# Order of the tail projections at the start of a segment-recurrent attention kernel, and a cap on the filling work of a step

## Chip, core and metric

The kernel runs on one core of one Trainium2 chip. The metric is the device time of one execution in microseconds (us). Before the change three timed runs gave 980.9, 981.39 and 983.57 us, so the median is 981.39 us.

The engines are named as in the profile: PE is TensorE (PEld its weight loads), ACT is ScalarE, DVE is VectorE, POOL is GpSimd, and SP is SyncE, which here does nothing but issue DMA transfers. PSUM is the memory that PE accumulates into; DVE and ACT copy ("evacuate") results from it to SBUF, the working memory.

## What is computed

Part A is attention with a memory that is carried from segment to segment. The sequence has 2048 tokens of 640 values, cut into 64 segments of 32. Each segment's 32 tokens stand behind 8 memory rows; the output of those 8 rows is the memory of the next segment. Part B is a dense layer with a squared ReLU. Layer norms and residuals stand around both.

```
mem = mem0                                   # 8 rows of 640
for s in range(64):
    h = concatenate([mem, xs], axis=1)       # 8 + 32 rows, xs = layernorm(x) of segment s
    q, k, v = h @ Wq, h @ Wk, h @ Wv         # 32 heads of 128
    scores = where(mask, q @ k.T * scale, -1e9)
    o = softmax(scores) @ v @ Wo
    mem = o[:, :8]
    outs.append(o[:, 8:])
h = x + concatenate(outs)
out = h + relu(layernorm(h) @ w1 + b1) ** 2 @ w2 + b2
```

Weights and activations are bfloat16, sums are float32.

## The kernel before

**Steps, blocks and tails.** A step is one segment; a block is four of them (128 tokens), so there are 16 blocks and 64 steps. A step's memory rows and its first 24 tokens are one group of 32 rows, projected inside the step (`step`, `proj`). The last 8 tokens of the four segments of a block form another group of 32 rows, the block's tail. Tails don't depend on the recurrence, so they can be projected at any time before their block: `tail_units(b, which)` cuts the projection of block b's tail by Wq, Wk or Wv into ten units of four matmuls, five for each half n of the heads. The last unit of a half hands out `tail_out`, the evacuation. The output projection of a block's tail rows is cut into ten units too (`wo_tail_units`).

**Evacuation and rows.** `tail_out` copies the half from PSUM to a row of 512 values per partition. A query or key half takes a row buffer from `rowtile` (four buffers, shared with the projections of the steps) and leaves a flip (a DVE transpose) in the list `late`, which frees the row. A value half is written to DRAM (`vt_d`) by a DMA transfer on SP, and its buffer is free when that transfer has landed. At the start 18 other places stand ready for value halves in the list `parked` (tiles that are needed only later, plus `parkx`), some with their writes put off in the list `writes`; value halves that find `parked` empty take a row buffer. Block 0's value halves take row buffers too and are written by POOL's queue. With blocks 1 to 9 parked, those of blocks 10 and 11 take row buffers.

**The start.** `start` streams Wv, Wq and Wk as they arrive, with tail units between the chunks. In the stream of wq and right behind it run the value units of blocks 4 to 7, 40 units. In the stream of wk run 30 units and right behind it ten more: value units of blocks 8 to 11. What is left in `units`, the tail queries and keys of block 1, goes into the list `fill` for step 0. All loads of weights stand on SP's queue in the order Wv, Wq, Wk, Wo (lines 114 and 149), and the writes of the parked values behind them.

**Step 0.** `step` runs with `ready` set: its projections are done already, by `start`. After the scores it runs ten units of `fill` and all flips in `late`, then the values and the copies of their result into oT. Wo comes in eight pieces, and the output rounds (`wo_rounds`, tile pw) of step 0 are in four parts that each need two pieces. `SEG0` says how many units of `fill` run ahead of each of the four parts. `wo_out` and `mem_to_hT` (line 374) then make the memory rows of the next step.

**Filling the later steps.** Ahead of each step `portion(s)` takes units from a plan that is sorted by due step. It aims at eight units a step on average from step 2 on (`n = round(8.0 * (s - 2)) - paced[0]`), always takes what is due, and can take only what is ready: when too little was ready in earlier steps, n is larger and a later step gets more than eight. The units run at four places of the step: one or two ahead of the memory's values, two behind them, two behind the output rounds, and the rest behind the token values, ahead of the next step's first projection.

**Semaphores of SP.** In the built program the transfers on SP use eight completion semaphores in turn, and each issue waits for the transfer eight issues before it.

Of the kernel before, what the change touches and what calls it, by code (L numbers as in the profile page):

```python
# [16 lines left out]
def kernel(  # L17
# [151 lines left out]
    def rows_of(b, sp):  # L169
        at = HD + sp * SEG  # L170
        return lambda c: hTs[b % 2][:, c * CW + at:c * CW + at + SEG]
# [15 lines left out]
    def ln_norm(b):  # L187
        mv, rs = xns[b]
        xn = s1.tile([128, D], BF16, tag="xn", name="xn")
        xt = xts.pop(b)  # L190
        nc.vector.tensor_scalar(out=xn[:], in0=xt[:], scalar1=mv[:, 0:1], scalar2=rs[:, 0:1],
                                op0=ALU.subtract, op1=ALU.mult)
        xns[b] = xn
# [28 lines left out]
    def proj(w, by, lhs, n, ps, c0, c1):  # L222

        if by == "columns":
            wr = w[:].rearrange("p (c g j n k e) -> p c n k g j e", c=DC, g=G, n=2, j=4, k=4)
        elif by == "half":
            wr = w[:].rearrange("p (c k j n e) -> p c n k j e", c=DC, k=G, n=2, j=4)
        else:
            wr = w[:].rearrange("p (c k n f) -> p c n k f", c=DC, k=G, n=2)
        for c in range(c0, c1):  # L230
            for k in range(4):
                nc.tensor.matmul(ps[32 * k:32 * k + 32, :], lhsT=lhs(c), rhs=wr[:, c, n, k], start=(c == 0), stop=(c == DC - 1))  # L232

    def mmtile():
        return mm.tile([128, 512], F32, tag="mm", name="ps")
# [4 lines left out]
    def evac(dve, out_, in_):  # L240
        if dve:
            nc.vector.tensor_copy(out=out_, in_=in_)  # L242
        else:
            nc.scalar.copy(out=out_, in_=in_)  # L244

    def rowtile():
        return s2.tile([128, 512], BF16, tag="row", name="row", bufs=4)
# [12 lines left out]
    def wo_rounds(lhs, pw, hs):  # L260

        for h in hs:
            for kh in range(2):
                for ch in range(2):
                    j = kh * 2 + ch
                    p = kh * 16 + h
                    c0 = 32 * (1 - kh)
                    nc.tensor.matmul(pw[32 * j:32 * j + 32, c0:c0 + DH], lhsT=lhs(p), rhs=wov2[:, head(p), ch],  # L268
                                     start=(h == 0), stop=(h == 15))
# [18 lines left out]
    def run(q, n, held=None, stop=False):  # L288
        while n > 0 and q:
            out = q.pop(0)()  # L290
            if out and held is not None:
                held.append(out)
                if stop:
                    break
            elif out:
                out[1]()
            n -= 1
# [15 lines left out]
    def tail_rows(b, c):  # L313
        return hTts[b // 4][:, c, b % 4].rearrange("p k s -> p (k s)")

    def tail_units(b, which):
        w = {"q": wq, "k": wk, "v": wv}[which]
        lhs = lambda c: tail_rows(b, c)
        st = {}

        def unit(n, c):
            def f():
                if c == 0:
                    st[n] = mmtile()
                proj(w, "columns" if which != "v" else "order", lhs, n, st[n], c, c + 1)
                return (True, lambda: tail_out(b, which, n, st[n][:])) if c == DC - 1 else None
            return f
        return [unit(n, c) for n in range(2) for c in range(DC)]

    def tail_out(b, which, n, ps, dve=False):  # L330
        row, wait = parked.pop(0) if which == "v" and 0 < b and parked else (rowtile()[:], False)
        evac_row(which, row, ps, dve)
        if which == "v":
            eng = nc.sync if b else nc.gpsimd

            def write():
                eng.dma_start(out=vt_d[b, 2 * n:2 * n + 2].rearrange("j r f -> r j f"),
                              in_=row.rearrange("r (j f) -> r j f", j=2))
            if wait:
                writes.append(write)  # L340
            else:
                write()
            return
        if n == 0:
            tails.setdefault(b, {})[which] = s2.tile([128, H, 32], BF16, tag=which + "Tt", name=which + "Tt")
        dst = tails[b][which]
        late.append((0.71, lambda: flip(row, dst, n), 4 * b - (which == "k")))
# [97 lines left out]
    def step(b, sp, v=None):  # L445
# [199 lines left out]
        if not last:  # L645
            pw = chn.tile([128, 512], F32, tag="ch", name="pw")
            if ready:
                for k in range(4):
                    run(fill, SEG0[k])
                    wo_rounds(lambda p: oT[:, p, M:NK], pw, [2 * k + h + 4 * (k // 2) for h in (0, 1, 4, 5)])  # L650
# [72 lines left out]
    parked += [(hnT0[:, c, :], True) for c in range(DC)] + [(ht0[k][:, 0:512], True) for k in range(NK4)]  # L723
    parked += [(t, True) for t, _ in halves(oTts[1][:].rearrange("p h r -> p (h r)"))]
    writes = []
    SEG0 = (0, 0, 8, 8)
    hnTs = [hnT0[:], ck(DC * NT).rearrange("p (c t) -> p c t", c=DC)]
    ots = [ck(D) for _ in range(4)]
    fxs = [ck(D) for _ in range(4)]
# [45 lines left out]
    def start():  # L775

        v = s2.tile([128, EG], BF16, tag="v", name="v")
        main = rows_of(0, 0)
        pas = [pop.tile([128, 2, 512], F32, tag="po%d" % h, name="pa%d" % h) for h in range(2)]
        banks = [pas[h][:, n, :] for h in range(2) for n in range(2)]  # L780
        banks += [mmtile()[:] for _ in range(3)] + [chn.tile([128, 512], F32, tag="ch", name="pv")[:]]
        for c in range(DC):
            for k in range(4):
                for n in range(2):
                    proj(wv, "order" if k else "half", (lambda c, b=k - 1: tail_rows(b, c)) if k else main, n,
                         banks[2 * k + n], c, c + 1)
        for n in range(2):
            evac(n == 1, v[:, n * 512:(n + 1) * 512], banks[n])
        for k in range(1, 4):
            for n in range(2):  # L790
                tail_out(k - 1, "v", n, banks[2 * k + n], n == 1)
        units = tail_units(3, "v")
        run(units, DC)
        ln_transpose(("t", 1))()
        ln_norm(("t", 2))
        run(units, DC)
        units += [u for b in range(4, 8) for u in tail_units(b, "v")]

        def stream(which, w, dst, turn=None):
            pas = [pop.tile([128, 2, 512], F32, tag="po%d" % h, name="pa%d" % h) for h in range(2)]  # L800
            for c in range(DC):
                for n in range(2):
                    proj(w, "columns", main, n, pas[0][:, n, :], c, c + 1)
                for n in range(2):
                    proj(w, "columns", lambda c: tail_rows(0, c), n, pas[1][:, n, :], c, c + 1)
                if c == 2 and turn:
                    turn()
                if c < DC - 1:
                    run(units, 7 + c % 2)
            run_late(0, 100)  # L810
            for n in range(2):
                row = rowtile()[:]
                evac_row(which, row, pas[0][:, n, :])
                tail_out(0, which, n, pas[1][:, n, :])
                flip(row, dst, n)
                run_late(0, 100)
                if which == "k":
                    tails_in(0, 0, n)

        stream("q", wq, qT, lambda: ln_transpose(("t", 2))())  # L820
        for n in range(2):
            spread(n)
        tails_v_in(0, nc.gpsimd, 0, 1)
        run(units, 10)
        parked.append((s1.tile([128, D], BF16, tag="xn", name="parkx")[:, 0:512], False))
        units += [u for b in range(8, 12) for u in tail_units(b, "v")]
        stream("k", wk, kT)
        units += tail_units(1, "q") + tail_units(1, "k")
        run(units, 10)
        fill.extend(units)  # L830
        return v
# [28 lines left out]
    for b in range(2, NB):  # L860
        for which in "qk":
            u = tail_units(b, which)
            plan += [(4 * b - 3 + (which == "k"), 4 * b - 5, u[DC * n:DC * n + DC]) for n in range(2)]
    for b in range(12, NB):
        u = tail_units(b, "v")
# [6 lines left out]
    def portion(s):  # L872
        n = round(8.0 * (s - 2)) - paced[0]
        got = []
        while True:
            if not begun:
                ready = [p for p in plan if p[1] <= s]
                if not ready:
                    break
                plan.remove(ready[0])  # L880
                begun.append(ready[0])
            d, _, u = begun[0]
            if len(got) >= n and d > s:
                break
            got.append(u.pop(0))
            if not u:
                begun.pop()
        paced[0] += len(got)
        return got
# [57 lines left out]
    for t in range(S // NT):  # L947
        hnT = hnTs[t % 2]
        more = t + 1 < S // NT
        got, hts, mvs = {}, {}, {}  # L950
        if t == 0:
            got = got1
# [3 lines left out]
        for fc in range(FC):  # L956
# [13 lines left out]
            if more and fc >= 1 and (fc - 1) // 3 < NK4:  # L970
                k, stage = divmod(fc - 1, 3)
# [30 lines left out]
        for q in range(NK4):  # L1002
# [6 lines left out]
            for hh in range(2):  # L1009
                k = pr + 2 * hh  # L1010
# [44 lines left out]
```

## Time and profile before

| | |
|---|---|
| median of three timed runs | 981.39 us |
| the profiled execution, its own time | 980.93 us |
| span of the profiled execution | 979.1 us |
| PE busy | 939.5 us, 96% |
| PEld busy | 547.4 us, 56% |
| DVE busy | 652.7 us, 67% |
| ACT busy | 525.1 us, 54% |
| POOL busy | 282.1 us, 29% |
| mean granted clock of PE | 0.995 |
| time up to the memory rows of step 1 (first row of line 374 after the streams) | 72.69 us |
| steps 1 to 62, from there | to 837.75 us |

Times in the views count from the start of the span. In a row of a timeline the first number is the start, the second the duration of the group; in square brackets stands how long the engine was idle ahead of it and what ended that. SPq rows are the issuing of a transfer, not its run; the chain of waits shows the run as DMA. A row of the table of windows gives the stretch, the busy time of PE, PEld, DVE, ACT and POOL with the number of instructions in brackets, then the granted clock of PE as a share of full speed, the share of the DMA engines, and GB/s.

### The profile page before, as it was taken

The page shows a single profiled execution, that of the slowest core. Times are in us where ns is not written, and L with a number is a line of the kernel's source. Part 1 is how long each engine was busy: PE and PEld are TensorE (multiplying, and loading weights), DVE is VectorE, ACT ScalarE, POOL GpSimd, SP SyncE. Part 2 cuts the span into 40 slices and gives each one's busy share as a digit, 9 for nine tenths or more (in the row PEclk, how much of TensorE's full clock was granted, in tenths as well). Part 3 has the DMA queues.
Part 4 walks back from the last instruction along what each step waited for, and adds up shares of the span by engine and source line. Part 5 has one row for each costly group of instructions (what it writes and reads, how often), then busy time and mean ns, then how long its engine had stood idle before and what let it go on. Part 6 is the DMA issues. An engine that isn't in the chain of part 4 may idle for free.

```text
span 979.1 us, 55574 instructions
## 1 busy us (share of the span) xinstructions
PE 939.5 (96%) x24760; PEld 547.4 (56%) x24760; DVE 652.7 (67%) x1942; ACT 525.1 (54%) x1271; POOL 282.1 (29%) x870
## 2 busy tenths in 40 slices
PE   6948999999999999999999999999999999999998
PEld 2425555555555555555555655555555656555555
DVE  5137777777676767776767676777776787566542
ACT  2425555566556556566656565665655655523321
POOL 2112323233223232323232323232323233263210
PEclk9979999999999999999999999999999999999999
DMA  9980110101010201010101010101010211543320
GB/s 355 400 273 28 14 31 9 30 15 31 14 37 14 31 13 31 9 31 8 31 14 31 14 31 11 33 12 33 11 33 6 53 40 24 165 137 79 98 55 27
DMA packets 65871, 56.62 MB, mean 58 GB/s; under 512 B 37384, under 2 KB 61712, under 8 KB 63712
## 3 DMA queue, kind: packets, MB, share of 16 engines
q1 hardware_dynamic: 65392, 52.74, 19.3%
q8 instruction: 194, 3.18, 1.4%
q14 instruction: 45, 0.37, 0.1%
q0 software_dynamic: 224, 0.33, 0.1%
q10 hardware_dynamic: 16, 0.01, 0.0%
HBM read 38.37 MB, written 9.44 MB: 49 GB/s over the span
## 4 chain that ended last, share of the span: by engine, by line
PE 84%; DVE 6%; DMA 4%; ACT 3%; SPq 2%; issue 1%; POOL 0%; ACTq 0%; DVEq 0%
PE ps L232 26%; PE pw L268 16%; PE px L232 12%; PE pq L232 7%; PE y L1012 6%; PE ps L960 6%; PE ps L268 3%; PE po L522 2%; DMA wq<-in_A_Wq_dram 2%; PE po L415 2%; SPq L149 2%; DVE kT L476 1%; PE sm L486 1%; DMA wo<-in_A_Wo_dram 1%; PE ps L575 1%
## 5 line engine op out<-in xcount | busy, mean ns | idle before, releaser
L232 PEld LDWEIGHTS <-hT 128*32 128x32 bf16 x7680 | 193.7, 96 | 189.9 <-DVE hT L374 23.2
L268 PE MATMUL pw<-wo,oT 128*32 128x320 bf16 x4224 | 161.9, 301 | 13.1 <-DVE oT L242 11.2
L232 PE MATMUL ps<-wk,hT 128*32 128x512 bf16 x2520 | 157.8, 379 | 0.0
L268 PEld LDWEIGHTS <-oT 128*32 128x32 bf16 x4224 | 118.9, 97 | 53.1 <-DVE oT L242 28.8
L256 DVE STREAM_TRANSPOSE qT<-row 128x512 bf16<-128x512 bf16 x128 | 90.7, 709 | 58.4 <-ACT row L251 55.0
L639 POOL TENSOR_TENSOR pkt<-ek,rk 128x64 bf16<-128x64 bf16 x64 | 18.9, 296 | 284.1 <-DVE rk L637 284.1
L232 PE MATMUL ps<-wv,hT 128*32 128x512 bf16 x1260 | 89.7, 378 | 0.0
L232 PE MATMUL pq<-wq,hT 128*32 128x512 bf16 x1260 | 79.5, 381 | 8.6 <-DVE hT L374 6.3
L244 ACT CAST row<-ps 128x512 bf16<-128x512 f32 x105 | 61.7, 590 | 37.8 <-PE ps L232 37.3
L426 ACT CAST oT<-po 128x512 bf16<-128x512 f32 x128 | 68.7, 589 | 20.4 <-PE po L420 18.9
L232 PE MATMUL px<-wq,hT 128*32 128x512 bf16 x1260 | 79.0, 379 | 0.0
L232 PE MATMUL px<-wv,hT 128*32 128x512 bf16 x1260 | 79.0, 378 | 0.0
L434 POOL COPY qz<-qT 128x96 bf16<-128x96 bf16 x126 | 33.6, 267 | 154.8 <-DVE qT L256 154.8
L968 ACT ACTIVATE wv<-ps,b1f 128x512 bf16<-128x512 f32 (+1 forms) x56 | 37.6, 672 | 66.6 <-PE ps L960 65.3
L633 ACT ACTIVATE ek<-tk 128x320 bf16<-128x320 f32 x64 | 30.1, 471 | 74.9 <-DVE tk L628 66.5
L256 DVE STREAM_TRANSPOSE kT<-row 128x512 bf16<-128x512 bf16 x65 | 46.2, 711 | 32.2 <-ACT row L244 32.0
L232 PEld LDWEIGHTS <-hTt 128*32 128x32 bf16 x1920 | 46.2, 96 | 27.9 <-issue 2.3
L1012 PE MATMUL y<-wq,wk 128*128 128x320 bf16 x416 | 58.9, 299 | 0.2
L473 ACT CAST row<-ps 128x256 bf16<-128x256 f32 x126 | 40.8, 375 | 28.5 <-PE ps L232 28.5
L251 ACT ACTIVATE row<-px 128x512 bf16<-128x512 f32 x63 | 37.6, 597 | 30.2 <-PE px L232 30.2
L486 PEld LDWEIGHTS <-qz 128*32 128x32 bf16 x2016 | 34.8, 94 | 32.4 <-POOL qz L436 3.7
L251 ACT ACTIVATE row<-pq 128x512 bf16<-128x512 f32 x63 | 37.6, 597 | 25.5 <-PE pq L232 25.0
(129 smaller groups left out, 1674.7 us busy)
## 6 DMA issues: line engine op xcount, KB each, us to landing
wv<-in_A_Wv_dram SPq DMA_DIRECT2D x5, 1024.0 KB
wq<-in_A_Wq_dram SPq DMA_DIRECT2D x5, 1024.0 KB
wk<-in_A_Wk_dram SPq DMA_DIRECT2D x5, 1024.0 KB
wo<-in_A_Wo_dram SPq DMA_DIRECT2D x8, 640.0 KB
o_all<-o SPq DMA_DIRECT2D x256, 7.5 KB
vt<-vt_d SPq DMA_DIRECT2D x60, 64.0 KB
xt<-in_A_x_dram SPq DMA_DIRECT2D x19, 160.0 KB
wq<-in_B_w_dram SPq DMA_DIRECT2D x1, 2080.0 KB
```

The source lines that it names most:

```text
L232: nc.tensor.matmul(ps[32 * k:32 * k + 32, :], lhsT=lhs(c), rhs=wr[:, c, n, k], start=(c == 0), stop=(c == DC - 1))
L244: nc.scalar.copy(out=out_, in_=in_)
L251: nc.scalar.mul(out=row, in_=ps, mul=scale)
L256: nc.vector.transpose(out=dst[:, n * 16:(n + 1) * 16, 0:32], in_=row.rearrange("p (h e) -> p h e", e=32))
L268: nc.tensor.matmul(pw[32 * j:32 * j + 32, c0:c0 + DH], lhsT=lhs(p), rhs=wov2[:, head(p), ch], start=(h == 0), stop=(h == 15))
L426: nc.scalar.copy(out=oTg[:, gs, :, 0:SEG], in_=po[1][h][:, :, 0:256].rearrange("p g (i q) -> p g i q", q=32))
L434: nc.gpsimd.tensor_copy(out=d.rearrange("p a (j f) -> p a j f", j=3)[:, :, :, 0:M], in_=src[:, :, 0:3, :])
L473: nc.scalar.copy(out=row[:, u * 256:(u + 1) * 256], in_=ps[:, u * 256:(u + 1) * 256])
L486: nc.tensor.matmul(sm[32 * g:32 * g + 32, 0:NK], lhsT=qz[:, p, :], rhs=kT[:, p, :], start=(j == 0), stop=(j == 3), skip_group_check=True)
L960: nc.tensor.matmul(ps[:], lhsT=w1[:, c, fc * 128:(fc + 1) * 128], rhs=hnT[:, c, :], start=(c == 0), stop=(c == DC - 1))
L968: nc.scalar.activation(out=r[:, 0:w], in_=ps[:, 0:w], func=ACT.Relu, bias=b1f[:, fc:fc + 1], scale=1.0)
L1012: nc.tensor.matmul(y[hh][:, 0:DH], lhsT=f1T[:, fc, k * 128:(k + 1) * 128], rhs=w2[:, fc, cs], start=(fc == 0 and not hf), stop=(fc == FFUL ...
```

## The change

Three edits. In the start, the units of block 1's tail queries and keys are exchanged with the value units of blocks 10 and 11: the stream of wk now carries values of blocks 8 and 9 and block 1's queries, block 1's keys run right behind the stream, and the values of blocks 10 and 11 are the `fill` of step 0. `SEG0` puts one of step 0's units ahead of the second part of the output rounds. In `portion`, no step is given more than nine units unless they are due.

```diff
-    SEG0 = (0, 0, 8, 8)
+    SEG0 = (0, 1, 8, 9)
...
         tails_v_in(0, nc.gpsimd, 0, 1)
         run(units, 10)
         parked.append((s1.tile([128, D], BF16, tag="xn", name="parkx")[:, 0:512], False))
-        units += [u for b in range(8, 12) for u in tail_units(b, "v")]
+        units += [u for b in (8, 9) for u in tail_units(b, "v")] + tail_units(1, "q")
         stream("k", wk, kT)
-        units += tail_units(1, "q") + tail_units(1, "k")
+        units += tail_units(1, "k") + [u for b in (10, 11) for u in tail_units(b, "v")]
         run(units, 10)
         fill.extend(units)
...
             d, _, u = begun[0]
-            if len(got) >= n and d > s:
+            if len(got) >= min(n, 9) and d > s:
                 break
```

In the built program the numbers of instructions on PE, 49522, and on POOL are the same before and after. On SP the four row writes of blocks 10 and 11 move behind four hnT writes, the load of block 1's x and four loads of block 0's tail values.

## The prediction

> **What bounds the kernel now.** I read four views: the table of windows for the first 120 us, the chain of waits and the timeline for 44 to 76 us, and the timeline of VectorE for line 374, which gives one row for each step of the recurrence. In the windows TensorE is busy 10.00 of 10 us from 30 to 50 us, then 3.96 and 4.40 of 10, then 8.46. So the front has one hole, between 50 and 73 us. The chain says what fills it:
>
> ```profile
> 47.80 2.30 SPq L149
> 50.14 10.31 DMA wo<-in_A_Wo_dram
> 60.51 2.84 DMA vt_d<-row
> 64.06 1.30 DVE qTt L256 x2
> 65.60 2.32 PE pw L268 x17
> ```
>
> The last piece of Wo lands at 60.45; the chain then goes through a write from a row buffer, then two flips, and only then do the output rounds (pw, line 268) begin. The timeline shows who waits:
>
> ```profile
> 52.91 2.35 PE L232 MATMUL ps<-wq,hTt 128*32 128x512 bf16 x40
> ...
> 60.51 1.95 SPq L337 DMA_DIRECT2D vt_d<-row  x4
> 62.52 2.10 SPq L337 DMA_DIRECT2D vt_d<-hnT  x4
> 63.43 1.08 ACT L251 ACTIVATE row<-ps 128x512 bf16<-128x512 f32 x2 [9.89 <-DMA vt_d<-row]
> 64.06 1.30 DVE L256 STREAM_TRANSPOSE qTt<-row 128x512 bf16<-128x512 bf16 x2 [9.70 <-ACT row L251]
> ...
> 64.67 0.48 SPq L120 DMA_DIRECT2D xt<-in_A_x_dram  x1
> 65.26 2.77 SPq L394 DMA_DIRECT2D vt<-vt_d  x4
> ...
> 65.60 2.32 PE L268 MATMUL pw<-wo,oT 128*32 128x320 bf16 x32 [9.96 <-DVE oT L242]
> ```
>
> Block 1's tail queries are multiplied at 52.91, but ScalarE cannot evacuate them for 9.89 us, because all row buffers hold values of blocks 10 and 11 or are in use, and those rows' writes stand on SP's queue behind Wo. ScalarE and VectorE work in order, so the copies of oT queue behind these rows and flips, and TensorE stands still 9.96 us.
>
> **The change, first part: the swap.** Work is conserved: 20 units of four matmuls change places with 20 others, one unit being 2.29/10 = 0.23 us (the ten units from 52.91 to 55.20). The queries of block 1 now come in the stream of wk and its keys behind it, at sites where TensorE is already full, so nothing is gained or lost there; two flips (0.67 us each) enter ahead of the kT flip at 48.85. The last of these two rows would be evacuated by 48.33, like the value row it replaces, so its flip ends near 49.0 and costs 0.15 us at most, which the later wait for Wo hides.
>
> In step 0 the ten units at 52.91 are now block 10's values. Their rows find buffers that flips, not transfers, release. ScalarE: second row from 55.3 to 55.9, then oT (0.27) to 56.2. VectorE: two key flips from 54.36 to 55.7, then oT (0.25). So the output rounds start at about 56.3. Each round of 16 matmuls takes 2.37/4 = 0.59 us (the x64 groups) and needs two pieces of Wo. In the built program an SP transfer waits for the one eight issues before it, so the parked writes date the pieces: the writes issued from 51.94 to 58.76 show pieces 1 to 7 landed by then. Rounds and fill: 0.59 + one unit + 0.59 + eight units + 0.59 + one unit = 4.1 us, to 60.4, when the last pieces are just there (60.45); the last round ends at 61.1 instead of 71.55. From there to the first projection of step 1 it was 73.09 - 71.55 = 1.54 us: 62.6 instead of 73.09.
>
> But the four row buffers are now the late thing. The built program lets the first three rows of step 1 wait for writes of blocks 10 and 11, and these four writes have moved on SP behind four hnT writes, the load of x and four loads of vt. SP is held by Wo until 60.51 as before. From there, by the rows above: four writes 2.0, one load 0.6, four loads 2.8, so the first row write is issued at 65.95. How long it takes is bounded by 2.84 us (the same transfer at 60.51, behind the parked writes) and 1.89 us (the load of mem0 on an empty queue at 1.21 us, in the chain); the page's 6.6 us for the row writes on POOL's queue is the far end. I take 2.84, the same transfer on the same queue: 68.8 us. What is queued behind that ScalarE row is all of step 1: the flips, the scores, the exponentials. The rows follow at 0.6 us each, VectorE's flips at 0.71: the flips run from 69.5 and the keys' first half is done at 70.9, the second at 72.65. The second scores, at 78.81 before, can start there: **6.15 us gained**. With 1.89 it would be 7.1; with 6.6, 2.4.
>
> TensorE meanwhile finishes the four projections (73.09 to 77.42 before, 4.33 us) at 67.0 and stands idle until 70.95, 3.95 us. The granted clock in windows of 0.25 us shows what idling did before:
>
> ```profile
> 58.00:58.25 0.25, 0.00 (x0) 0.00 (x0) 0.00 (x0) 0.00 (x0) 0.00 (x0) 1.00 1.10 349
> 58.25:58.50 0.25, 0.00 (x0) 0.00 (x0) 0.00 (x0) 0.00 (x0) 0.00 (x0) 0.65 1.10 336
> 58.50:58.75 0.25, 0.00 (x0) 0.00 (x0) 0.00 (x0) 0.00 (x0) 0.00 (x0) 0.50 1.11 349
> ```
>
> The last matmul had ended at 55.64, so the clock fell to half after 2.75 us, and came back at 68.6, 3.0 us after work resumed at 65.60. If it falls here, the 24 value matmuls ahead of the second scores take 2.6 us instead of 1.3, which makes those scores some **1.1 us** later. I charge it, because 3.95 is above the 2.75 seen. [...]
>
> Sum of this part: 6.15 - 1.1 = 5.05 us.
>
> **Second part: the cap.** Following the planner's arithmetic, the fill of steps 7, 11 and 15 goes from 10, 12 and 14 units to 9, and the moved units make eleven steps (7, 8, 11, 12, 13, 15 to 20) nine units long; step 61 gives one of ten to step 62, which had none. From step 21 to 60 nothing differs. Durations come from the distance of successive hT rows:
>
> ```profile
> 244.56 0.34 DVE L374 STREAM_TRANSPOSE hT<-o 128x160 bf16<-128x160 bf16 x1
> 257.16 0.35 DVE L374 STREAM_TRANSPOSE hT<-o 128x160 bf16<-128x160 bf16 x1
> 270.31 0.35 DVE L374 STREAM_TRANSPOSE hT<-o 128x160 bf16<-128x160 bf16 x1
> ...
> 677.66 0.35 DVE L374 STREAM_TRANSPOSE hT<-o 128x160 bf16<-128x160 bf16 x1
> 689.86 0.34 DVE L374 STREAM_TRANSPOSE hT<-o 128x160 bf16<-128x160 bf16 x1
> 701.96 0.34 DVE L374 STREAM_TRANSPOSE hT<-o 128x160 bf16<-128x160 bf16 x1
> ```
>
> Steps with no fill (1 and 2) and many with eight units take 12.09 us: eight units lie in the shadow of the step's chain. Fourteen units made step 15 last 12.60 and pushed step 16 to 13.15, 1.57 us over the floor in all; twelve cost 0.27 + 0.57 = 0.84 (steps 11, 12), ten 0.32 + 0.14 = 0.46 (steps 7, 8): 2.87 us to be saved. The only nine-unit step, 50, took 12.20 and the one after it 12.10, so a ninth unit costs 0.12; eleven of them 1.3 us. The far end is a whole unit, 0.23 each, 2.6 us. I take the row of the same size: **1.6 us gained** (between 0.3 and, if a ninth unit were free, 2.9). Step 61 I cost at nothing: its unit falls in step 62, where no fill stands.
>
> **Sum.** The profiled execution took 980.93 us (span 979.1 and 1.83 around it); the three timed runs have a median of 981.39, 0.05% more, which I leave aside. 980.93 - 5.05 - 1.6 = 974.3 us.
>
> **The rivals.**
> (a) The clock does not fall in step 1: 974.3 - 1.1 = 973.2. For it: the gap is only 3.95 us, and four dense projections come just before it, while the fall seen followed several shorter gaps. Against: 3.95 is longer than 2.75.
> (b) Nine-unit steps cost the whole unit: 980.93 - 5.05 - 0.3 = 975.6. For it: step 8 before, with eight units, was already 0.14 over the floor. Against: step 50.
> (c) The rows land late, after 6.6 us: 2.4 - 1.1 = 1.3 gained in front, 978.0. For it: POOL's row writes. Against: those had 16 busy DMA engines beside them, while the DMA share at 66 to 68 us is 0.44.
> (d) Slower: moved units upset the steps they land in. Steps 23, 24, 39 and 40 exceed the floor by 0.82 to 0.89 us with eight units, with gaps ahead of matmuls that the waits put down to issue alone (0.59 us at 551.23). If all eleven nine-unit steps took 12.94, they would cost 9.4 us against 2.9 saved: 980.93 - 5.05 + 6.5 = 982.4. It decides from 0.98 us a step. Against: such steps are 4 of 62.
> (e) The front gives everything back, because block 1's rows still wait as they did: about 979.3. The built program speaks against it: their copies there wait for no transfer.
>
> **Chances.** Forecast 0.42, (a) 0.25, (b) 0.13, (c) 0.10, (d) 0.05, (e) 0.05. What a measurement tells from no change is about 0.3%, 2.9 us, so below 978.45 counts as faster: the forecast, (a), (b) and most of (c), 0.90. Same takes the rest of (c), (e) and part of (d): 0.07; slower 0.03. The range reaches down below (a) by the 0.95 us that a landing after 1.89 us would add and part of a free ninth unit, and up to just short of (c): 971.8 to 977.8.
>
> **What would show it.** In the new profile: ScalarE's rows of block 1's queries not waiting for a transfer; the output rounds of step 0 starting at 56 to 57 us and ending at about 61; the first row of step 1 waiting 4 to 5 us for a write of row, until near 68.8; the clock at 0.5 around 70.5 us; hT rows 12.2 us apart in steps 7 to 20, and no 13.15. I am wrong if the output rounds wait for something else until past 65, or if the hT row of step 2, at 96.87 before, comes later than 93.5 or earlier than 89.

## The result and the profile after

Four runs of the changed kernel gave 971.71, 973.64, 974.14 and 974.41 us, so the median is 973.89 us. The runs of the kernel before on the same chip had a median of 981.42 us. The ratio is 0.992 with a 95% interval of 0.9907 to 0.9933, that is 6.6 to 9.1 us less. The forecast was 974.3 us in a range of 971.8 to 977.8.

| | before | changed |
|---|---|---|
| median | 981.42 us | 973.89 us |
| the profiled execution, its own time | 980.93 us | 971.71 us |
| its span | 979.1 us | 969.6 us |
| PE busy | 939.5 us | 937.7 us |
| hT row (line 374) at the end of step 0 | 72.69 us | 64.88 us |
| at the end of step 3 | 109.08 us | 102.90 us |
| from there to the end of step 6 | 36.28 us | 36.29 us |
| steps 7 to 20 | 173.78 us | 173.07 us |
| steps 21 to 62 | 518.61 us | 515.98 us |
| from there to the end of the span | 141.35 us | 141.36 us |

The profiled execution of the changed kernel is the fastest of its four, so its span shows more gain (9.5 us) than the medians do (7.5 us). Steps 0 to 3 give 6.2 us of it, and steps 7 to 20 give 0.7. Of steps 21 to 62, which give the other 2.6 us, only the last two have another plan; they are taken up in the section on why the prediction was right.

The chain of waits of the changed kernel from 50 to 72 us (start, duration, what) shows what sets the start of step 1 now:

```profile
50.09 10.29 DMA wo<-in_A_Wo_dram
60.40 0.36 SPq L337
...
62.97 0.51 SPq L120
...
63.58 0.76 SPq L394
...
66.45 2.50 DMA vt_d<-row
...
69.05 0.61 ACT row L251
69.68 0.71 DVE qT L256
70.39 0.60 DVE kT L256
71.04 0.28 PE sm L486 x16
```

Wo still lands at 60.4. But what follows it in the chain is no longer the output projection of step 0. SP issues the hnT writes, block 1's x and the four vt loads, and only then, at 66.45, the first write of a row buffer. That buffer is what step 1's first row on ScalarE waits for, until 69.05.

The timeline of the same stretch has the rows that answer to those shown of before:

```profile
52.22 2.33 PE L232 MATMUL ps<-wv,hTt 128*32 128x512 bf16 x40
...
55.35 0.83 PE L268 MATMUL pw<-wo,oT 128*32 128x320 bf16 x16 [0.42 <-DVE oT L242]
...
58.31 0.61 PE L232 MATMUL ps<-wv,hTt 128*32 128x512 bf16 x2 [2.02 <-issue]
...
62.82 0.92 PE L268 MATMUL pw<-wo,oT 128*32 128x320 bf16 x16
...
65.28 1.26 PE L232 MATMUL pq<-wq,hT 128*32 128x512 bf16 x20 [1.53 <-DVE hT L374]
...
66.45 2.64 SPq L337 DMA_DIRECT2D vt_d<-row  x4
...
69.05 0.60 ACT L251 ACTIVATE row<-pq 128x512 bf16<-128x512 f32 x1 [4.57 <-DMA vt_d<-row]
...
71.04 0.28 PE L486 MATMUL sm<-kT,qz 128*32 128x40 bf16 x16 [1.26 <-DVE kT L256]
...
72.43 0.28 PE L486 MATMUL sm<-kT,qz 128*32 128x40 bf16 x16
```

Where TensorE stood still for 9.96 us ahead of pw, it now waits 0.42 us. Two things are new. TensorE stops for 2.02 us in the middle of the output rounds and waits for nothing that the profile shows ("issue"). And ScalarE waits 4.57 us for a transfer in step 1. TensorE feels only 1.26 us of the second, because its projections began at 65.28 and run beside it.

The windows of the changed kernel around these rounds (busy time of the five engines, then granted clock, DMA share and GB/s) show a third thing:

```profile
57.50:57.75 0.25, 0.00 (x0) 0.00 (x0) 0.21 (x2) 0.00 (x0) 0.00 (x0) 1.00 1.04 358
57.75:58.00 0.25, 0.00 (x0) 0.00 (x0) 0.19 (x1) 0.00 (x0) 0.00 (x0) 0.83 1.11 374
...
61.00:61.25 0.25, 0.25 (x8) 0.18 (x4) 0.00 (x0) 0.00 (x0) 0.00 (x0) 0.50 0.51 152
61.25:61.50 0.25, 0.25 (x11) 0.10 (x4) 0.00 (x0) 0.00 (x0) 0.00 (x0) 0.84 0.93 275
```

The granted clock is at half from 57.92 to 61.33, in step 0 rather than in step 1, where it stays at 1.00.

The rows of line 374 on VectorE, here the ends of steps 14 to 17, answer to those that showed the dear step 16:

```profile
238.17 0.34 DVE L374 STREAM_TRANSPOSE hT<-o 128x160 bf16<-128x160 bf16 x1
250.42 0.34 DVE L374 STREAM_TRANSPOSE hT<-o 128x160 bf16<-128x160 bf16 x1
263.18 0.34 DVE L374 STREAM_TRANSPOSE hT<-o 128x160 bf16<-128x160 bf16 x1
275.58 0.34 DVE L374 STREAM_TRANSPOSE hT<-o 128x160 bf16<-128x160 bf16 x1
```

Steps 15, 16 and 17 take 12.25, 12.76 and 12.40 us, where they took 12.60, 13.15 and 12.10.

### The profile page after: what moved, and what is told of

The parts are those of the page before. It is cut to its first block, busy times and chain, and to the rows that moved or that the text cites. A ratio compares the mean times of both kernels' runs of the same rounds, so it can differ in the third digit from the quotient of the medians.

```text
span 969.6 us, 55554 instructions
## 1 busy us (share of the span) xinstructions
PE 937.7 (97%) x24749; PEld 546.9 (56%) x24760; DVE 652.6 (67%) x1942; ACT 524.5 (54%) x1271; POOL 280.5 (29%) x870
## 3 DMA queue, kind: packets, MB, share of 16 engines
q8 instruction: 194, 3.18, 1.4%
## 4 chain that ended last, share of the span: by engine, by line
PE 85%; DVE 5%; DMA 4%; SPq 2%; ACT 2%; issue 1%; POOL 0%; ACTq 0%; DVEq 0%; POOLq 0%
PE ps L232 27%; PE pw L268 15%; PE px L232 13%; PE pq L232 7%; PE y L1012 6%; PE ps L960 6%; PE ps L268 3%; PE po L522 2%; DMA wq<-in_A_Wq_dram 2%; PE po L415 2%; SPq L149 2%; PE sm L486 1%; PE ps L575 1%; DMA wo<-in_A_Wo_dram 1%; DVE kT L476 1%
```

## The experiments

Chips differ by up to 0.2% in the time of the kernel before, so each run is compared by its ratio to that kernel on its own chip. The last four columns come from one profile each. The ratio, with its interval, is the recorded one; it is not the quotient of the two medians, from which it differs by up to 0.0013 (in e1).

| run | median, us | before, same chip | ratio (95%) | hT, step 0 | step 1 | step 3 | steps 7 to 20 |
|---|---|---|---|---|---|---|---|
| changed | 973.89 | 981.42 | 0.992 (0.9907 to 0.9933) | 64.88 | 78.38 | 102.90 | 173.07 |
| e1_swap_only | 976.49 | 981.52 | 0.9936 (0.9918 to 0.9955) | 66.31 | 79.62 | 104.14 | 173.95 |
| e2_cap_only | 979.78 | 981.52 | 0.9986 (0.9975 to 0.9996) | 73.60 | 85.70 | 110.00 | 172.70 |
| e3_parked | 976.13 | 981.52 | 0.9935 (0.9917 to 0.9953) | 64.36 | 79.23 | 103.54 | 174.66 |
| e4_rows_first | 973.41 | 981.52 | 0.9908 (0.989 to 0.9927) | 65.23 | 77.37 | 101.90 | 173.71 |
| e5_no_cap | 974.29 | 979.26 | 0.9948 (0.9933 to 0.9962) | 64.90 | 79.27 | 103.80 | 173.95 |
| e6_shift | 973.68 | 979.26 | 0.9947 (0.9933 to 0.9961) | 62.97 | 81.62 | 106.14 | 171.61 |
| e7_rows_first_shift | 970.24 | 979.26 | 0.9906 (0.9891 to 0.9921) | 62.74 | 76.28 | 100.81 | 172.37 |
| e8_changed_again | 972.69 | 979.65 | 0.9935 (0.9921 to 0.995) | 64.64 | 79.21 | 103.74 | 172.55 |
| e9_rows_and_shift | 971.64 | 979.65 | 0.9921 (0.9905 to 0.9937) | 62.98 | 77.96 | 105.23 | 172.01 |
| e10_loads_first | 971.84 | 980.11 | 0.9917 (0.9904 to 0.9931) | 64.36 | 76.50 | 101.03 | 173.25 |
| e11_loads_first_shift | 968.50 | 980.11 | 0.9885 (0.9871 to 0.9898) | 62.71 | 75.33 | 99.84 | 172.57 |

**The swap alone and the cap alone.** e1 is the changed kernel without the cap and with the old SEG0:

```diff
-    SEG0 = (0, 1, 8, 9)
+    SEG0 = (0, 0, 8, 8)
...
-            if len(got) >= min(n, 9) and d > s:
+            if len(got) >= n and d > s:
```

> The exchange of the units alone: step 0's parts stay at (0, 0, 8, 8) and no step is capped. Theory A (the row buffers held by writes behind Wo made the hole in the front, and the exchange fills it): the front gains as in the changed kernel, 6.2 us by step 3, and the rest stays as before, so 975.2 us; the hT row of step 2 near 90.7 us, steps 15 and 16 again 12.6 and 13.1 us. Rival B (the gain is the cap's, and what the front gains is lost again in later steps): 979 us or more.

e2 is the kernel before with the cap:

```diff
-            if len(got) >= n and d > s:
+            if len(got) >= min(n, 9) and d > s:
```

> The cap of nine units alone, with the start as before. Theory A: what the steps 7 to 20 of the changed kernel's trace show, 0.7 us less than before, so 980.7 us (979.8 if a ninth unit costs only the 0.12 us seen in step 50, 981.1 if it costs a whole unit). Rival B (the cap makes the gain): 975 us or less.

The swap alone gives 6.3 us (4.4 to 8.1, from the ratio), the cap alone 1.4 us (0.4 to 2.4). They add up to 7.7 us, and the change gave 7.5. By the medians they would be 5.0 and 1.7 us, 6.8 together, each within its interval.

**Buffers or order?** e3 leaves the order of the units as it was before and gives the four value halves of blocks 10 and 11 places of their own, in tiles that are not in use yet:

```diff
+        kpark = s2.tile([128, H, 32], BF16, tag="kTt", name="parkk")[:].rearrange("p h r -> p (h r)")
+        parked.extend(halves(kpark))
+        parked.extend([(hTs[1][:, 0:512], False), (s2.tile([128, D], BF16, tag="xt", name="parkt")[:, 0:512], False)])
```

> The kernel before, with its order of units and of SP's transfers, but four more places to park the value halves of blocks 10 and 11, so that no row buffer is held by a transfer. Theory A: block 1's rows in step 0 wait for nothing, the output rounds start near 56 us instead of 65.6, and the first row of step 1 doesn't wait for a transfer either; the load of block 1's x, which still stands late on SP's queue and lands near 67 us, is late next and costs about 1 us. 974.5 us (973.5 to 976). Rival C (the hole is set by the landing of Wo or by the order on SP, and the row buffers only end it): 979 us or more, output rounds not before 63 us.

The ratio is that of the swap alone, 0.9935 against 0.9936. Block 1's query rows no longer wait for a transfer, though they stand where they stood before. So what the swap pays for is row buffers that no transfer holds; the order of the projections is only a way to get there. That the two ratios are equal is in part chance: e3's step 0 ends 2.0 us before that of e1, and its step 1 takes 1.6 us more. Step 1's first row doesn't wait for a transfer either. Something else does, as e3's timeline shows:

```profile
65.78 0.44 SPq L120 DMA_DIRECT2D xt<-in_A_x_dram  x1
66.13 0.60 ACT L251 ACTIVATE row<-pq 128x512 bf16<-128x512 f32 x1 [2.17 <-PE pq L232]
...
69.36 0.89 DVE L156 BATCH_NORM_STATS2 lnst<-xt 128x6 f32<-128x320 bf16 x2 [4.21 <-DMA xt<-in_A_x_dram]
...
71.16 0.60 ACT L251 ACTIVATE row<-px 128x512 bf16<-128x512 f32 x1 [3.06 <-DVE qT L256]
```

The load of block 1's x stands behind eight writes that follow Wo on SP, as before the change; in the changed kernel it stands behind four and is issued at 62.97. VectorE waits 4.21 us for it, with the flips of step 1 behind. Step 1 takes 14.87 us, 2.8 us over the 12.09 of before, where about 1 us was expected.

**The row writes earlier on SP.** e4 moves the load of x and the loads of block 0's values behind the flips of step 0, where block 10's row writes already stand ahead of them, and puts four of the writes that were put off, those of hnT, behind block 11's row writes, ahead of `wo_out`:

```diff
             run_late(0, 100)
+            load_x(1)
+            tails_v_in(0, nc.sync, 1, 4)
...
+            if ready:
+                run(writes, 4)
             o = wo_out(pw)
...
-            if b == 0:
+            if b == 0 and sp > 0:
                 run(writes, 4)
-            if b == 0 and sp == 0:
-                load_x(1)
-                tails_v_in(0, nc.sync, 1, 4)
```

> The changed kernel, but on SP's queue the row writes of block 10 stand ahead of the load of x and the tail values, and those of block 11 ahead of the four hnT writes. Theory A (in the changed kernel the start of step 1 is set by where the row writes stand on SP's queue): the first row of step 1 starts at about 66.6 us instead of 69.05, 2.4 us less than the changed kernel, so 971.5 us. Rival D (step 1 is held by something else at the same time, TensorE or VectorE, and the wait for the write covers it): 973.9 us, no change.

In the timeline of e4 the row no longer waits for the write:

```profile
65.63 1.26 PE L232 MATMUL pq<-wq,hT 128*32 128x512 bf16 x20 [1.53 <-DVE hT L374]
...
67.00 0.60 ACT L251 ACTIVATE row<-pq 128x512 bf16<-128x512 f32 x1 [2.15 <-issue]
```

Step 1 takes 12.14 us instead of the changed kernel's 13.50, so the wait for the row write cost 1.4 us there (2.2 and 2.4 us by the profiles of e5 and e8, which have the same front). Only 1.0 us of it is left at step 3, because e4's own step 0 ended 0.35 us later; 2.4 us had been expected. By the times the two kernels can't be told apart (0.9908 against 0.992, overlapping intervals).

**The cap out, all else kept.** e5 differs from the changed kernel by the line of the cap alone, as in e1.

> The changed kernel without the cap: exchange and the new parts (0, 1, 8, 9). It differs from the exchange alone (976.49 us) by the parts only, and from the changed kernel (973.89 us) by the cap only. Theory A: the new parts do nothing by themselves, the 1.2 us by which the exchange alone was behind in step 0 came from two windows of half clock instead of one; the cap is worth about 1.5 us as in the run of the cap alone: 975.4 to 976.5 us. Rival G (the new parts are worth the 1.2 us of step 0): 975.0 us or less, and the output rounds of step 0 again some 1.2 us ahead of those of the exchange alone.

It gains 5.1 us (3.7 to 6.6), and its step 0 ends at 64.90 like the changed kernel's 64.88. The new SEG0 is all that separates e5 from e1, and nothing in the ratios shows a gain from it: 0.9948 against 0.9936. Taken alone, 974.29 us would meet rival G's bound of 975.0, but the kernel before was 2.3 us faster on this chip than on that of e1. The 1.4 us by which e1's step 0 ended later go with the clock: half from 57.43 to 64.26 in e1, from 57.78 to 61.19 in e5. Whether the new SEG0 shortened that stretch, one profile of each doesn't show.

**What stops TensorE in the output rounds?** Up to the stop, the windows count the instructions that TensorE has run (busy time and, in brackets, matmuls, then the same of weight loads). Of the changed kernel:

```profile
0.00:58.00 58.00, 45.39 (x862) 21.86 (x863) 25.93 (x69) 23.71 (x43) 11.33 (x32) 1.00 0.99 376
```

of e1, where no unit stands between the first two parts of the rounds:

```profile
0.00:57.50 57.50, 45.04 (x862) 21.92 (x863) 25.66 (x68) 23.72 (x43) 11.40 (x32) 1.00 0.98 375
```

and of e3, where the order of the projections is another one and the rounds start 1.8 us later:

```profile
0.00:58.60 58.60, 46.20 (x862) 22.00 (x863) 24.01 (x65) 23.34 (x43) 11.38 (x32) 1.00 0.99 374
```

It is 862 matmuls and 863 weight loads each time, in e4, e5, e8 and e10 too, whatever these instructions are. e6 moves the place: 80 small matmuls of a piece of the identity, into a tile that nobody reads, run at the very start, ahead of TensorE's first transposes.

```diff
     load_w(wv, A_Wv, 3, 4)
+    dm = mm.tile([128, 512], F32, tag="mm", name="dm")
+    for _ in range(80):
+        nc.tensor.matmul(dm[0:32, 0:32], lhsT=ident[0:32, 0:32], rhs=ident[0:32, 0:32], start=True, stop=True,
+                         skip_group_check=True)
     ln_transpose(0)()
```

> The changed kernel with 80 small matmuls that nobody reads, in TensorE's idle time ahead of its first transpose: every later instruction of TensorE stands 160 places further on in its stream. Theory E (the stop of some 2 us after the 1724th instruction of TensorE in step 0 is a wait for the next block of instructions, which comes through the transfers of Wo): the stop again follows instruction 1724, which is now in the middle of block 10's units, some 3 us earlier in the program; it is shorter there, and the output rounds run without a stop and end near 61.5 us instead of 63.7. The total moves little, since the first row of step 1 waits for its write until 69 us all the same: 973 to 974.5 us. Rival F (the stop belongs to its place in the program, a wait for Wo or for a bank): it stays behind the first output round, and the rounds end near 63.7 us.

The stop of 2 us is gone from the rounds, and the shorter one that was expected behind the 862nd matmul doesn't show either. TensorE waits only 0.49 us, until 60.14, with these instructions run:

```profile
0.00:59.90 59.90, 50.99 (x990) 26.47 (x991) 25.85 (x69) 24.32 (x44) 12.10 (x34) 1.00 0.99 375
```

These are 128 matmuls and 128 weight loads more than the 862 and 863 of the other kernels, 256 instructions. In e7, e9 and e11, which have the 80 matmuls too, TensorE stops at the same count, for 0.49, 0.52 and 0.27 us. So in these eleven kernels the place of the stop went by the count of TensorE's instructions, and not by what the program does there.

Step 0 ends 1.9 us earlier, at 62.97. But step 1 takes 18.65 us. The timeline of e6 and its windows show why:

```profile
67.16 1.98 SPq L337 DMA_DIRECT2D vt_d<-row  x4
...
70.14 0.60 ACT L251 ACTIVATE row<-pq 128x512 bf16<-128x512 f32 x1 [7.56 <-DMA vt_d<-row]
...
72.12 0.32 PE L486 MATMUL sm<-kT,qz 128*32 128x40 bf16 x16 [4.25 <-DVE kT L256]
...
74.77 0.37 PE L486 MATMUL sm<-kT,qz 128*32 128x40 bf16 x16
```

```profile
70.00:70.25 0.25, 0.00 (x0) 0.00 (x0) 0.00 (x0) 0.11 (x1) 0.00 (x0) 1.00 0.85 232
70.25:70.50 0.25, 0.00 (x0) 0.00 (x0) 0.00 (x0) 0.25 (x1) 0.00 (x0) 0.61 0.96 289
...
76.75:77.00 0.25, 0.25 (x36) 0.24 (x28) 0.00 (x0) 0.10 (x1) 0.00 (x0) 0.50 0.85 262
77.00:77.25 0.25, 0.25 (x35) 0.20 (x20) 0.00 (x0) 0.25 (x1) 0.00 (x0) 0.74 0.30 100
```

The projections of step 1 end earlier, the row write doesn't (it is issued 0.7 us later than in the changed kernel, and the first row starts 1.1 us later), so TensorE is idle for 4.25 us and the clock is at half from 70.3 to 77.1. The second scores come 2.65 us after the first instead of 1.39. This is what the prediction had charged to the changed kernel. The earlier step 0 alone was worth nothing here; it made the next wait longer, 7.56 us where it was 4.57.

e7 takes the edits of e4 and e6 together.

> The same 80 matmuls in the kernel with the row writes of blocks 10 and 11 ahead on SP's queue. Theory E: now that no row waits for a write, the end of the output rounds sets the start of step 1; they end 2 us sooner, and the total is 2 us below the 973.41 us of the kernel with the rows ahead: 971.4 us. Rival F: 973.4 us, no change. It may also be that the third row of step 1, which waits for block 11's write, comes late then; that would leave about 1 us of the gain.

The ratio is 0.9906, and step 3 ends 2.1 us before that of the changed kernel. Of the 2 us that were expected against e4, the ratios show nothing (0.9906 and 0.9908, with intervals wider than that), and step 3 ends 1.1 us earlier, about what the expectation left for a late row of block 11. One wait is left in its step 1, for block 11's writes, which e4's order puts behind the loads:

```profile
68.21 0.60 ACT L251 ACTIVATE row<-px 128x512 bf16<-128x512 f32 x1 [2.05 <-DMA vt_d<-row]
```

e8 is the changed kernel once more, beside others on another chip.

> The changed kernel once more, on the chip of the next run and in a second profiled execution. Theories A and E: the steps 1 to 3 and 7 to 20 take the times they had, a stop of TensorE near 2 us follows its 1724th instruction, and the first row of step 1 waits for a write until about 69 us; 0.992 of the kernel before. The long steps behind step 21 fall elsewhere, since nothing there differs from the kernel before.

The stop is there again, 1.88 us behind the same 862nd matmul, but the clock doesn't fall in the front (its mean over the execution is 1.0, where it was 0.998 in the first profile). Step 1 takes 14.57 us and not the 13.50 of the first profile, since its first row waits until 69.89. The ratio, 0.9935, agrees with the first (0.992).

**The order of SP by what is needed next.** e9 has e6's 80 matmuls, a little later. It loads x behind the flips, and puts the loads of the values and the four hnT writes behind all four row writes, ahead of `wo_out`:

```diff
     mem_to_hT(o0, 0, 0)
+    dm = mm.tile([128, 512], F32, tag="mm", name="dm")
...
             run_late(0, 100)
+            load_x(1)
...
+            if ready:
+                tails_v_in(0, nc.sync, 1, 4)
+                run(writes, 4)
             o = wo_out(pw)
...
-            if b == 0:
+            if b == 0 and sp > 0:
                 run(writes, 4)
-            if b == 0 and sp == 0:
-                load_x(1)
-                tails_v_in(0, nc.sync, 1, 4)
```

> All four row writes ahead of the tail values on SP's queue, and the 80 unread matmuls between the first two groups of transposes, where TensorE waits for VectorE for 2.2 us, so that they don't put off the clock's rise at the start. Theories A and E together: no row of step 1 waits for a write, the output rounds of step 0 run without a stop of 2 us and end near 61 us, step 1 takes its 12.1 us and its hT row comes near 74.5 us instead of 78.4: 4 us less than the changed kernel on the same chip (3 to 5). If the rounds' stop were a wait for Wo, or the rows' wait only a cover for another one, 1.5 us or less.

It missed: the gain over the changed kernel on the same chip is 1.05 us where 4 were expected, and steps 1 and 2 take 15.0 us each. Five hnT writes and three ht writes, issued from 67.75 to 72.89, now stand ahead of the load of block 2's x, and the timeline of e9 shows VectorE waiting for it near the end of step 1, ahead of that step's hT row at 77.96:

```profile
72.99 1.74 SPq L120 DMA_DIRECT2D xt<-in_A_x_dram  x1
76.61 0.49 DVE L184 BATCH_NORM_STATS2 lnsx<-xt 128x6 f32<-128x320 bf16 x1 [2.96 <-DMA xt<-in_A_x_dram]
...
78.36 2.33 PE L232 MATMUL pq<-wq,hT 128*32 128x512 bf16 x20 [3.30 <-DVE hT L374]
```

Step 2 pays for that wait a second time: TensorE was idle for 3.30 us, the clock was at half from 77.1 to 84.0, and the first projection takes 2.33 us instead of 1.26.

e10 therefore runs the writes that nobody waits for behind each of the steps 1 to 3 and not ahead of it, and leaves the 80 matmuls out; e11 is e10 with them, where e9 had them.

```diff
             run_late(0, 100)
+            load_x(1)
...
+            if ready:
+                tails_v_in(0, nc.sync, 1, 4)
             o = wo_out(pw)
...
-            if b == 0:
-                run(writes, 4)
-            if b == 0 and sp == 0:
-                load_x(1)
-                tails_v_in(0, nc.sync, 1, 4)
...
             step(b, sp, v0 if b + sp == 0 else None)
+            if b == 0 and sp > 0:
+                run(writes, 4)
```

> The changed kernel with SP's queue in the order in which things are needed: row writes of block 10, x of block 1, row writes of block 11, tail values, x of block 2, tail values of block 1, and only then the eleven put-off writes, after the steps 1 to 3. No matmuls are added. Theory A: neither a row nor an x is waited for in the steps 1 and 2, step 1 takes 12.1 us as it did before the change and its hT row comes near 77 us (the rounds of step 0 still stop for 2 us); 1.5 us less than the changed kernel, 0.991 of the kernel before. Rival H (each wait taken off SP's queue is replaced by the next one, as x of block 2 was for 3.0 us in the last run): step 1 or 2 takes 13.5 us or more, 0.993.

> The same with the 80 unread matmuls between the first two groups of transposes, so that the wait for instructions falls ahead of the output rounds. Theories A and E together: the rounds end near 61.8 us, step 1 takes 12.1 us, its hT row comes near 75 us, 3.5 us less than in the changed kernel: 0.989 of the kernel before. Rival H: step 1 or 2 takes 13.5 us or more, 0.992.

Step 1 takes 12.14 us in e10. e11 is the fastest kernel of all: 968.50 us, 0.9885 (0.9871 to 0.9898), below the intervals of the changed kernel, of its repetition and of e10; the intervals of e4 and e7 still touch its own. Its timeline:

```profile
56.40 0.84 PE L268 MATMUL pw<-wo,oT 128*32 128x320 bf16 x16 [0.42 <-DVE oT L242]
...
60.49 2.15 SPq L337 DMA_DIRECT2D vt_d<-row  x2
...
63.11 1.26 PE L232 MATMUL pq<-wq,hT 128*32 128x512 bf16 x20 [1.53 <-DVE hT L374]
...
64.47 0.60 ACT L251 ACTIVATE row<-pq 128x512 bf16<-128x512 f32 x1 [2.16 <-PE pq L232]
65.09 0.89 DVE L156 BATCH_NORM_STATS2 lnst<-xt 128x6 f32<-128x320 bf16 x2 [1.58 <-DMA xt<-in_A_x_dram]
```

The row writes follow Wo at once, step 1's first row waits for its projection and nothing else, and what is left is 1.58 us for block 1's x. The 80 matmuls are worth 1.2 us at the end of step 3 (101.03 to 99.84), and the times give e11 3.3 us over e10; where the rest comes from these single profiles don't show.

## Why the prediction was right

**The swap: right in mechanism, but 5.05 us was some 1 us too low.** Three kernels have the changed front (changed, e5, e8); their step 3 ends at 103.5 us on average, against 109.5 in the two that have the old one (before, e2). That is 6.1 us; by the times e5 gives 5.1 (3.7 to 6.6) and e1 6.3 (4.4 to 8.1). Step by step:

- *Block 1's rows stop waiting for a transfer, the output rounds start at 56.3.* They started at 55.35. Right.
- *The rounds end at 61.1, the first projection comes at 62.6.* This step failed: they ended at 63.74, and the projection came at 65.28. The working took TensorE as free to run at full clock. It stopped 2.02 us behind its 862nd matmul, as in six other kernels, and in this stop the clock fell to half for 3.4 us.
- *The first row of step 1 waits for a row write until 68.8.* It started at 69.05. SP issued the write 0.5 us later than worked out, since the four hnT writes took 2.5 us and not 2.0, and it landed after 2.50 us instead of 2.84. The second scores came at 72.43, where 72.65 was expected: 6.4 us of gain, forecast 6.15.
- *1.1 us for a clock at half in step 1.* Not due: TensorE's idle time there was 1.26 us and not 3.95, because its projections were late (2.13 and 2.33 us in e5 and e8, where the clock stayed at full too). By the prediction's own row (0.65 between 58.25 and 58.50) the fall of before came 2.7 us after the last matmul and not 2.75, which changes nothing in the choice. Rival (a) had this point right, though for another reason than the one given. e6 shows that the charge itself was well sized: with step 0 ending at 62.97 the idle time was 4.25 us, the clock fell, and the second scores were 1.26 us late.

The first error cost nothing, because the row write, the later of the two, set the start of step 1 anyway, and it took the second error with it: the late projections kept TensorE busy. In e6, with the rounds on time, step 3 ends 3.2 us after that of the changed kernel. That the two errors cancelled is luck, and so is part of the nearness of the total: the forecast stands for 6.65 us less than the 980.93 of the profiled execution, rival (a) for 7.75, and the medians moved by 7.5. Counted from the median of 981.42, the forecast's gain would have ended at 974.8 and that of rival (a) at 973.7.

**The cap: right.** Steps 7 to 20 have one plan in all nine kernels with the cap, and another in all four without it. With it they took 171.61 to 173.71 us in the profiles, without it 173.78 to 174.66; the means are 172.65 and 174.08, so 1.4 us are saved. e2's times give 1.4 (0.4 to 2.4). The forecast was 1.6. The hT rows of the changed profile are 12.36 us apart there on average (12.41 before), not the 12.2 that was named as a sign. One profile of the changed kernel against one of before would have said 0.7. One small thing was taken as nothing and isn't: step 62 takes 12.31 to 12.45 us with the cap and 12.52 to 12.76 without. Without it step 61 has a tenth unit, which runs ahead of step 62's first projection.

**Steps 21 to 61** have one plan in all kernels up to 60, and step 61 differs by that one unit. They took 502.5 to 505.4 us in the nine profiles with the cap and 504.0 to 506.9 in the four without, and gaps put down to issue alone fall now here, now there (the last section has the packets that came ahead of them). The 2.4 us by which the profiles of before and changed differ there (506.09 and 503.66) are therefore not claimed for the change. Kernels with the cap lie lower on average; why is open.

**The rivals.** (b), a nine-unit step costs a whole unit: its saving of 0.3 us lies outside the 0.4 to 2.4 of e2, if narrowly. (c), rows land 6.6 us after issue: they took 2.50. (d), moved units upset the steps they land in: it needed 12.94 us in eleven steps, and the longest from 7 to 20 is step 16 with 12.76; the gaps that it pointed to are there in every kernel, but stay below 0.8 us each. (e), the front gives all back: no, block 1's rows waited for no transfer. By the times alone, forecast (974.3) and (a) (973.2) can't be told apart around 973.89; the trace decides, and for (a): the clock did not fall in step 1.

## What to carry to other kernels

A buffer that a transfer frees was held here as long as everything ahead of that transfer on its queue: with Wo, 5120 KB in eight pieces, ahead of the row writes, ScalarE waited 9.89 us for a row. To give such buffers to results that nobody is waiting for, or to put the values elsewhere, was worth the same (0.9936 in e1, 0.9935 in e3). Each wait that was taken away uncovered the next on the same queue (the row write, 4.57 us in the changed kernel; x of block 1, 1.58 us in e11; x of block 2, 2.96 us in e9), so the order of the whole queue is to be written by when each item is needed, and a stage that is only made earlier can end up later (in e6 step 0 ended 1.9 us earlier and step 3 3.2 us later). A part worth 1 us of 980 is sized by several profiles or several timed rounds, since single ones differed by more than that (step 1 of the same kernel took 13.50 and 14.57 us).

## What the runs showed of the hardware

**TensorE stopped at one count of instructions.** In seven kernels (changed, e1, e3, e4, e5, e8, e10) it stood still for 1.3 to 2.3 us in the output rounds with no wait in the profile, each time behind the 862nd matmul. The four kernels with 160 more instructions (80 matmuls and their weight loads) ahead of it didn't stop there, but 256 instructions further on, and for 0.5 us at most. In the changed kernel's stop the DMA share was 1.0 to 1.1, with Wo and the parked writes under way, and a packet of the instruction queue ran from 55.70 to 56.82 us; TensorE went on at 58.31, 1.49 us after its end. In all eleven kernels that stopped, it went on 1.2 to 1.6 us after such a packet had ended. The page of the profile counts 194 packets and 3.18 MB on that queue, 16.4 KB each. If all of them held TensorE's instructions, its 49522 over 194 packets would be 255 in each; that is an estimate, and the stop moved by 256. That TensorE waited there for instructions is an inference from this count and these times, and that they came late because the DMA engines were full is another; no run took the load of Wo away. Shorter stops, as long after a packet, come later, where the DMA engines have little to do (0 to 2 tenths from 73 to 824 us on the changed kernel's page): between 80 and 840 us of the thirteen profiles TensorE paused 39 times for 0.26 to 0.77 us within an output round, and each of these pauses ended 1.2 to 1.6 us after an instruction packet (the 0.59 us at 551.23 that the prediction names: 1.35 us).

**The clock stood at half for 3.4, 6.8 or 10.2 us.** From fall to rise it was 3.4 us in the changed kernel (57.92 to 61.33), e4 and e5, 6.8 in e1, e6 and e9, and 10.2 in before (58.32 to 68.56) and e2; in e3, e7, e8, e10 and e11 the front shows no fall. Why these are one, two and three times 3.4 us is not shown by any run. After the last matmul had ended the clock fell 1.65 us later in the changed kernel and 2.7 us later in before. And the same program fell in one profile and not in the other (e8), so that a single profile tells little of whether a short gap costs clock: idle times of 2.0 to 2.3 us did in the changed kernel, e1, e4 and e5, one of 2.49 us in step 1 of e3 did not.
